# A fused attention and SwiGLU block on one core: gate columns by crossbar-turned weights and VectorE sums, rows spread through DRAM

## The chip, the cores and the metric

The kernel runs on one core of one Trainium2 chip. The metric is the device time of one execution in microseconds (us). Before the change the median of three runs is 1275.24 us (1275.18 to 1275.56).

## The reference

One block of a transformer with conditioning (adaLN), cut to what matters:

```python
mod = (silu(c) @ w_mod).reshape(1, 6, 1, 1024)      # sa, ca, ga, sb, cb, gb
h = layernorm(x) * (1 + ca) + sa
x = x + ga * attention(h)        # wq; 32 query heads on 4 kv heads, last 512 keys; wo
h = layernorm(x) * (1 + cb) + sb
x = x + gb * ((silu(h @ w_gate) * (h @ w_up)) @ w_down)
```

x is 2048 x 1024 in bf16, c is 1 x 1024, w_mod is 1024 x 6144, wq is 1024 x 4096, wo is 4096 x 1024, and the feed-forward width is 3584. The six groups of 1024 numbers in `mod` are the shift, scale and gate of the attention half (sa, ca, ga) and of the feed-forward half (sb, cb, gb).

## The kernel before

**Tiling.** The 2048 rows are worked in four chunks of 512. Attention runs over 128 steps of one (chunk, head) pair each: the loop `for i in range(1, NA + 2)` at line 839, with the 32 heads of chunk 0 in steps 1 to 33. In the steady state step i holds, in TensorE's order, the query projection of head i+3 (`qproj`, eight matmuls of 512 columns into bank QB), the scores of head i-1 (`scores`, four matmuls into four banks, which two exponentials on ScalarE, line 757, empty) and the attention product of head i-2 (`pv`, sixteen matmuls of 129 columns into two banks). VectorE then copies the query projection out (line 640) and, after the product, takes the reciprocal of the sums (line 775) and multiplies (line 778); SyncE issues a crossbar transfer (DMA transpose) that turns the head's output (line 781). After a chunk's last head comes its output projection (`oproj`), whose result is multiplied by a gate row and added to x (`resid`, lines 797 and 799). After all four chunks come gate, up and down projections of the feed-forward half. Steps 1 to 8 are different: the first heads' projections were done before the loop, so that in the odd ones among them no query projection runs.

**Order.** Every engine's instructions are in the order in which the code emits them; there is no planner. `T.op` puts the waits ahead of an instruction by the buffers it reads and writes. SyncE is one in-order queue for nearly all loads, stores and turns: a load that waits holds those behind it. A list of generators, `bg`, gives one piece of background work to each step (`run_bg(1)`): `ln_task` normalises the next chunk in twelve pieces, three empty ones and four that scale and shift. For chunk 1 it starts in step 5.

**The six groups of mod.** sa and ca are made by TensorE at the start. The gate ga is made in chunk 0: two loads of w_mod (`load_wga`, line 562, 1 MB each, steps 2 and 3) and 64 matmuls with one column each (`mod_mm`, called at line 879, in steps 7, 9, 10, 11 and 12). The other three groups, sb, cb and gb, come as 24 columns of 128 in chunks 1 and 2: `load_mt` (line 580) brings a block of w_mod, 1024 x 128, by a DMA transpose into one of two buffers, and four steps later `mod_col` (line 585) multiplies it by the row silu(c) on VectorE and sums along the row.

**Rows.** The gates are needed as rows spread over all partitions (`rowb[0]` for ga, `rowb[1]` for gb), and `mod_col` needs silu(c) so (`sc_row`). `row_task` (line 594) makes such a row from a column tile: GpSimd multiplies the identity matrix by each column (line 600), TensorE multiplies a matrix of ones by these diagonals (eight matmuls of 128 columns in two halves), and VectorE copies the halves out (line 608). It is run three times.

**Loads beside.** In chunk 0 SyncE also issues a 1 MB block of wq every four steps (`load_wq`, line 354, in steps 4, 9, 13, 17, 21, 25 and so on), needed four steps later; eight 1 MB blocks of wo (line 791; steps 5, 7, 10, 12, 15, 18, 20, 23); and a chunk of x (line 299; step 19).

Of the kernel before, what the change touches and what calls it, by code (L numbers as in the profile page):

```python
# [3 lines left out]
ALU = mybir.AluOpType  # L4
AF = mybir.ActivationFunctionType
BF16 = mybir.dt.bfloat16
F32 = mybir.dt.float32
P = 128
# [122 lines left out]
def bass_adaLN_cond__sliding_block_cached__swiglu_ffn__prompt_kernel(  # L131
# [21 lines left out]
    DT = D // P  # L153
# [6 lines left out]
    NJ = 6 * DT  # L160
# [21 lines left out]
    c_row = S_("c_row", [DT, P], BF16)  # L182
    sc_bf = S_("sc_bf", [P, DT], BF16)
    mod_bf = S_("mod_bf", [P, NJ], BF16)
    c6 = S_("c6", [P, DT], F32)
    mcol = S_("mcol", [P, 3 * DT], F32)
    gain = [S_("gain%d" % i, [P, DT], BF16) for i in range(2)]
    gain_f = S_("gain_f", [P, DT], F32)
    nmean = S_("nmean", [P, 1], F32)
# [11 lines left out]
    KB = 1024  # L201
# [7 lines left out]


    OFF_H20 = 154 * KB
    B_ident = _Buf("ident"); B_ones = _Buf("ones"); B_zw = _Buf("zw")
    B_diag = [_Buf("diag%d" % i) for i in range(4)]
    ident = arena.at(OFF_H20, [P], BF16, [B_ident])
    ones_bf = arena.at(OFF_H20 + 256, [P], BF16, [B_ones])
    diag = [arena.at(OFF_H20 + 512 + 256 * i, [P], BF16, [B_diag[i]]) for i in range(4)]
    zwarm = arena.at(OFF_H20 + 2048, [512], BF16, [B_zw])

    def bank(b, n=512, off=0):
        return ps[:, b * 512 + off:b * 512 + off + n]  # L220
# [10 lines left out]
    PB = [_Buf("bank%d" % b) for b in range(8)]  # L231
    B_x = [_Buf("x%d" % t) for t in range(ST)]
    B_mh = _Buf("mhalf")
    B_cT = _Buf("cT"); B_sc = _Buf("sc"); B_late = [_Buf("late%d" % i) for i in range(4)]; B_c6 = _Buf("c6"); B_mcol = _Buf("mcol"); B_scr = _Buf("scr")
    B_mode = _Buf("mode"); B_modc = _Buf("modc"); B_bq = _Buf("bq"); B_gf = _Buf("gf")
    B_nm = _Buf("nmean"); B_acc = _Buf("acc"); B_acc0 = _Buf("acc0")
    B_g = [_Buf("g%d" % i) for i in range(2)]
# [18 lines left out]
    XB = 7  # L256

    with nc.Block() as block:

        @block.gpsimd  # L260
        def _(g):
# [5 lines left out]
            def mm(out_ap, lhsT, rhs, start, stop, reads, bank_buf, skip=False):  # L267
                T.op(PE, lambda: TE.matmul(out_ap, lhsT, rhs, start=start, stop=stop, skip_group_check=skip),  # L268
                     reads=reads, writes=[bank_buf])
# [15 lines left out]
            def finish(gen):  # L285
                while gen in bg:
                    run_bg(1)
# [3 lines left out]
            T.op(POOL, lambda: g.affine_select(out=ident, in_=ident, compare_op=ALU.not_equal,  # L291
                                               fill=1.0, base=0, pattern=[[-1, P]], channel_multiplier=1),
                 reads=[B_ident], writes=[B_ident])
            T.op(POOL, lambda: g.memset(ones_bf, 1.0), writes=[B_ones])
            T.op(POOL, lambda: g.memset(mhalf[:, :], -0.5), writes=[B_mh])
            T.op(POOL, lambda: g.memset(zwarm, 0.0), writes=[B_zw])

            def load_x(ch):
                T.op(Q_x[TPC + ch], lambda: SP.dma_start(
# [156 lines left out]
            def mod_mm(w_ap, wbuf, k, cols):  # L456
                for n, (j, o) in enumerate(cols):
                    mm(bank(XB, 1, 2 * o), w_ap[:, j * P:(j + 1) * P], sc_bf[:, k:k + 1],
                       k == 0 and n == 0, k == DT - 1, [wbuf, B_sc], PB[XB], skip=True)
# [35 lines left out]
            def mod_ca(hf, k):  # L495
# [5 lines left out]
            T.op(PE, lambda: TE.transpose(bank_bf(XB)[:, 0:DT], c_row[:, :], ident[0:DT, 0:DT]),  # L501
                 reads=[B_cT, B_ident], writes=[PB[XB]])
            T.op(ACT, lambda: A.activation(sc_bf[:, :], bank_bf(XB)[:, 0:DT], AF.Silu), writes=[PB[XB], B_sc])
            T.op(ACT, lambda: A.activation(acc[:, 0:1], mhalf[:, 0:1], AF.Exp), reads=[B_mh], writes=[B_acc])


# [47 lines left out]
            norm(2, 2, 2, 512, 512)  # L554


            B_wga = [_Buf("wga%d" % k) for k in range(DT)]
            wga = arena.at(OFF_WO + 48 * KB, [DT, D], BF16, B_wga)
            GCOLS = [(j, j) for j in range(DT)]

            def load_wga(i):
                T.op(dq("q_wga%d" % i), lambda: SP.dma_start(
                    wga[:, i * HK:(i + 1) * HK, :],
                    w_mod[i * HK * P:(i + 1) * HK * P, NE * P:NE * P + D].rearrange("(k p) n -> p k n", p=P)),
                     writes=B_wga[i * HK:(i + 1) * HK])

            NF = NE + DT
            NL = NJ - NF  # L570
            B_mt = [_Buf("mt%d" % i) for i in range(2)]
            mt = [arena.at(OFF_H20 + (2 + 2 * i) * KB, [D], BF16, [B_mt[i]]) for i in range(2)]
            sc_row = arena.at(OFF_H20 + 6 * KB, [D], BF16, [B_scr])
# [2 lines left out]
            def load_mt(n):  # L576
                if n < 2:
                    for b_ in B_qT[NQT:]:
                        B_mt[n].absorb(b_)
                T.op(Q_mt[n % 2], lambda: SP.dma_start_transpose(  # L580
                    mt[n % 2].rearrange("p (a b) -> p a b", a=1), w_mod[:, (NF + n) * P:(NF + n + 1) * P]),
                     writes=[B_mt[n % 2]])

            def mod_col(n):
# [2 lines left out]
                     reads=[B_scr], writes=[B_mt[n % 2], B_mcol])  # L587

            def mod_take(g0, cbuf):
                T.op(DVE, lambda: V.tensor_copy(mod_bf[:, NF + g0 * DT:NF + (g0 + 1) * DT], mcol[:, g0 * DT:(g0 + 1) * DT]),  # L590
                     reads=[B_mcol], writes=[cbuf])


            def row_task(dst, dbuf, src, sbuf):
                T.op(POOL, lambda: g.tensor_copy(c6[:, :], src), reads=[sbuf], writes=[B_c6])

                def diags(n):
                    for q in range(4):
                        col = 4 * n + q
                        T.op(POOL, lambda: g.tensor_scalar(diag[q], ident, c6[:, col:col + 1], None, op0=ALU.mult),  # L600
                             reads=[B_ident, B_c6], writes=[B_diag[q]])

                diags(0)
                yield
                for n in range(2):
                    for q in range(4):
                        mm(bank(XB, P, q * P), ones_bf, diag[q], q == 0, q == 3, [B_ones, B_diag[q]], PB[XB], skip=True)
                    T.op(DVE, lambda: V.tensor_copy(dst[:, n * 512:(n + 1) * 512], bank(XB)),
                         writes=[PB[XB], dbuf])
                    if n == 0:  # L610
                        diags(1)
                    yield


            LEAD = 3
            NQT = 5; NEX = 2; NOS = 4
# [211 lines left out]
            def add_ln2(ch):  # L828
                s = ch % 2
                if ch == 0:  # L830
                    finish(rows)
                    h2s[0] = arena.at(OFF_H20, [DT, CH], BF16, B_h2[0])
                ln2[ch] = ln_task(ch, h2s[s], B_h2[s], 1, 3 * DT, B_late[1])
                bg.append(ln2[ch])

            LOADX = {19: 2, 40: 3}
            LOADT = {Hq + 2 + (9 * n) // 4: n for n in range(NL)}
            LOADO = {5 + (21 * p) // 8: p for p in range(8)}
            for i in range(1, NA + 2):
                ch, h = divmod(i, Hq)  # L840
# [1 line left out]
                    load_wq((i + 4) // 4 + 1)  # L842
                if 2 <= i < NQ0:
                    q_shifted(i)
                if i in (2, 3):
                    load_wga(i - 2)
                if i in LOADX:
                    load_x(LOADX[i])
                if i in LOADO:
# [1 line left out]
                for gk in {2: (1,), 3: (2,), 4: (3,)}.get(i, ()):  # L851
# [3 lines left out]
                    if gk == Hkv - 1:  # L855
                        for b_ in B_hT[1]:
                            for kb in B_kn:
                                b_.absorb(kb)
                if i == 17:
                    bg.append(row_task(sc_row, B_scr, sc_bf[:, :], B_sc))  # L860
                if i == 5:
                    add_ln1(1)
                if h == 2 and 1 <= ch < NCH - 1:
# [3 lines left out]
                if i + LEAD < NA:  # L867
# [7 lines left out]
                        qproj(i + LEAD)  # L875
                    elif i % 2 == 0:
                        qproj(NQ0 - 1 + i // 2)
                for k in {7: (0, 1, 2, 3), 9: (4,), 10: (5,), 11: (6,), 12: (7,)}.get(i, ()):
                    mod_mm(wga[:, k, :], B_wga[k], k, GCOLS)
                    if k == DT - 1:  # L880
                        T.op(DVE, lambda: V.tensor_copy(mod_bf[:, NE:NF], psap(XB * 512, [[2, DT]])), writes=[PB[XB], B_late[0]])
                        rows = row_task(rowb[0], B_row[0], mod_bf[:, NE:NF], B_late[0])
                        bg.insert(0, rows)
                if i - 4 in LOADT:
                    n = LOADT[i - 4]
                    mod_col(n)
                    g0, last = divmod(n, DT)
                    if last == DT - 1:
                        mod_take(g0, B_late[g0 + 1])
                        if g0 == 1:  # L890
                            mod_gain(1, B_late[2], B_g[1])
                        elif g0 == 2:
                            rows = row_task(rowb[1], B_row[1], mod_bf[:, 5 * DT:6 * DT], B_late[3])
                            bg.insert(0, rows)
                if i in LOADT:
                    load_mt(LOADT[i])
                n = i - (NA - LEAD)
# [6 lines left out]
                if 0 <= i - 2 < NA:  # L904
                    pv(i - 2)
                    ch2, h2 = divmod(i - 2, Hq)
                    if h2 == Hq - 1 and ch2 < NCH - 1:
                        finish(rows)
                        oproj(ch2)
                run_bg(1)  # L910

# [148 lines left out]
```

## Time and profile before

| what | value |
|---|---|
| median of three runs | 1275.24 us |
| span of the profiled execution | 1273.8 us |
| TensorE busy, share of the span | 1267.0 us, 99% |
| VectorE / ScalarE / GpSimd busy | 479.6 / 341.5 / 42.0 us |
| DMA, mean | 122 GB/s |
| mean granted TensorE clock | 1.000 |
| a steady attention step | 3.50 us |

A timeline line of the profile reads: start in us from the start of the span, length in us, engine, source line, operation, what it writes and reads, shape, how many are merged, and in brackets how long the engine sat idle before it and what ended that. PE is TensorE's matmuls, PEld its weight loads, DVE is VectorE, ACT is ScalarE, POOL is GpSimd, SPq is SyncE's queue. Matmuls are recorded with overlapping lengths, so their spacing is read from their starts. "Idle before" is only a loss on the engine that sets the end.

### The profile page before, as it was taken

How to read it: one execution, taken by the hardware profiler on the slowest of the kernel's cores; microseconds unless marked ns; L12 is line 12 of the kernel's file. 1: busy time of each engine (PE TensorE's matmuls, PEld its weight loads, DVE VectorE, ACT ScalarE, POOL GpSimd, SP SyncE). 2: the span in 40 equal slices, each digit the busy share in tenths (PEclk: the TensorE clock that was granted, in tenths of full speed). 3: DMA queues.
4: the chain of work that ended last, by engine and by line, in shares of the span. 5: the costliest groups of instructions: out<-in, count | busy, mean ns of one | idle time of the engine just before them, and what ended most of it. 6: DMA issues, size and time to landing. Idle time of an engine off the chain costs nothing.

```text
span 1273.8 us, 17943 instructions
## 1 busy us (share of the span) xinstructions
PE 1267.0 (99%) x7683; PEld 645.7 (51%) x7683; DVE 479.6 (38%) x897; ACT 341.5 (27%) x388; POOL 42.0 (3%) x102
## 2 busy tenths in 40 slices
PE   8999999999999999999999999999999999999999
PEld 5665545555455564455544444444444444444444
DVE  4655315764147652365322331233212331222222
ACT  4555304554025550155510111011100111011100
POOL 1020000000000010000000000000000000000000
PEclk9999999999999999999999999999999999999999
DMA  9999403876018641055253973056411644035200
GB/s 306 271 235 224 99 1 84 194 169 133 1 34 191 140 104 38 5 129 118 67 147 99 285 222 121 25 154 152 148 60 56 192 140 132 17 120 161 66 9 25
DMA packets 235854, 155.31 MB, mean 122 GB/s; under 512 B 129024, under 2 KB 222080, under 8 KB 235776
## 3 DMA queue, kind: packets, MB, share of 16 engines
q1 hardware_dynamic: 177520, 95.45, 30.7%
q10 hardware_dynamic: 58256, 58.73, 14.7%
q8 instruction: 60, 0.98, 0.3%
q14 instruction: 18, 0.15, 0.0%
HBM read 119.54 MB, written 4.19 MB: 97 GB/s over the span
## 4 chain that ended last, share of the span: by engine, by line
PE 99%; DMA 1%; DVE 0%; SPq 0%; ACT 0%; issue 0%
PE ps L268 98%; DMA arena<-in_A_wq_dram 1%; DVE arena L671 0%; SPq L331 0%; SPq L306 0%; PE ps L272 0%; ACT arena L757 0%; DVE arena L666 0%; DVE tmp L797 0%; DVE arena L799 0%; DVE bq L661 0%
## 5 line engine op out<-in xcount | busy, mean ns | idle before, releaser
L268 PE MATMUL ps<-arena 128*128 128x512 bf16 (+1 forms) x7378 | 1260.7, 334 | 4.0 <-POOL arena L408 2.2
L268 PEld LDWEIGHTS ps<-arena 128*128 128x128 bf16 x7378 | 635.6, 98 | 621.0 <-issue 3.9
L757 ACT ACTIVATE arena<-ps 128x1024 bf16<-128x1024 f32 x256 | 261.9, 1023 | 350.3 <-PE ps L268 338.4
L989 ACT ACTIVATE arena<-ps 128x512 bf16<-128x512 f32 x112 | 66.9, 597 | 506.4 <-PE ps L268 506.4
L990 DVE TENSOR_TENSOR arena<-ps,arena 128x512 bf16<-128x512 f32 x112 | 77.4, 691 | 276.6 <-PE ps L268 276.6
L797 DVE TENSOR_TENSOR tmp<-ps,rowb 128x512 f32<-128x512 f32 (+1 forms) x65 | 44.4, 683 | 318.8 <-PE ps L268 318.8
L640 DVE CAST arena<-ps 128x512 bf16<-128x512 f32 x120 | 82.9, 691 | 53.8 <-PE ps L268 53.8
L778 DVE TENSOR_TENSOR arena<-ps,rl 128x512 bf16<-128x512 f32 x128 | 88.5, 691 | 4.7 <-DVE rl L775 0.3
L775 DVE RECIPROCAL rl<-ps 128x4 f32<-128x4 f32 x128 | 23.3, 182 | 118.3 <-PE ps L268 118.3
L415 DVE BATCH_NORM_STATS2 st<-x_res 128x6 f32<-128x512 bf16 x62 | 42.3, 683 | 3.6 <-DMA x_res<-in_A_x_dram 3.5
L420 POOL TENSOR_SCALAR rstd<-mv 128x1 f32<-128x1 f32 x28 | 6.3, 226 | 888.2 <-DVE mv L419 888.2
L585 DVE SCALAR_TENSOR_TENSOR arena<-arena 128x1024 bf16<-128x1024 bf16 x24 | 29.1, 1214 | 0.0
L799 DVE TENSOR_TENSOR arena<-tmp,x_res 128x512 bf16<-128x512 f32 (+1 forms) x33 | 22.3, 675 | 1.1
L799 DVE TENSOR_TENSOR x_res<-tmp,x_res 128x512 bf16<-128x512 f32 x32 | 22.1, 692 | 1.1
L431 DVE TENSOR_SCALAR arena<-arena,gain,mod_bf 128x512 bf16<-128x512 bf16 x56 | 20.3, 404 | 0.0
L426 DVE TENSOR_SCALAR nsc<-x_res,mv,rstd 128x1024 bf16<-128x1024 bf16 x30 | 16.0, 533 | 0.0
L422 POOL TENSOR_TENSOR rstd<-rstd,mhalf 128x1 f32<-128x1 f32 x28 | 15.8, 564 | 2.3
L600 POOL TENSOR_SCALAR arena<-arena,c 128x128 bf16<-128x128 bf16 x24 | 14.4, 616 | 32.7 <-PE ps L268 32.4
L268 PEld LDWEIGHTS ps<-sc_bf,arena 128*128 128x128 bf16 x192 | 6.6, 96 | 2.3 <-DMA arena<-in_w_mod_dram 0.3
L268 PE MATMUL ps<-sc_bf,arena 128*128 128x1 bf16 x192 | 6.8, 163 | 0.0
L419 DVE BATCH_NORM_AGGREGATE mv<-st 128x2 f32<-128x12 f32 x28 | 5.8, 209 | 1.0
L653 DVE COPY arena<-ps 128x512 f32<-128x512 f32 x4 | 2.7, 688 | 8.3 <-PE ps L268 8.3
(53 smaller groups left out, 50.7 us busy)
## 6 DMA issues: line engine op xcount, KB each, us to landing
arena<-in_A_wq_dram SPq DMA_DIRECT2D x31, 1024.0 KB, 6.1
arena<-in_B_w_gate_dram ACTq DMA_DIRECT2D x28, 1024.0 KB, 5.4
arena<-in_B_w_up_dram ACTq DMA_DIRECT2D x28, 1024.0 KB, 8.1
arena<-in_A_wo_dram SPq DMA_DIRECT2D x8, 1024.0 KB, 6.4
arena<-in_B_w_down_dram SPq DMA_DIRECT2D x7, 1024.0 KB, 8.4
out_dram<-arena SPq DMA_DIRECT2D x15, 256.0 KB, 2.0
x_res<-in_A_x_dram SPq DMA_DIRECT2D x3, 1024.0 KB, 6.7
arena<-in_w_mod_dram SPq DMA_DIRECT2D x8, 256.0 KB, 6.3
```

What stands on the lines that cost most here:

```text
L268: T.op(PE, lambda: TE.matmul(out_ap, lhsT, rhs, start=start, stop=stop, skip_group_check=skip), reads=reads, writes=[bank_buf])
L415: T.op(DVE, lambda: V.bn_stats(st_[sl][:, hf * 6:hf * 6 + 6], x_res[:, t, hf * 512:hf * 512 + 512]), reads=[B_x[t]], writes=[B_st[sl]])
L431: T.op(DVE, lambda: V.tensor_scalar(dst[:, dt, :], dst[:, dt, :], gain[gi][:, dt:dt + 1], mod_bf[:, ccol + dt:ccol + dt + 1], op0=ALU.mult ...
L585: T.op(DVE, lambda: V.scalar_tensor_tensor(mt[n % 2], mt[n % 2], 1.0, sc_row, op0=ALU.mult, op1=ALU.mult, accum_out=mcol[:, n:n + 1]), rea ...
L640: T.op(DVE, lambda: V.tensor_copy(qT_s[qs], bank(b)), writes=[PB[b], B_qT[qs]])
L757: T.op(ACT, lambda: A.activation(ex_s[es][:, 2 * kp:2 * kp + 2, :], banks2(SCB + 2 * kp), AF.Exp, scale=att_scale), writes=[PB[SCB + 2 * k ...
L775: T.op(DVE, lambda: V.reciprocal(rl[r][:, :].rearrange("p (a b) -> p a b", a=2), psap(PVB * 512 + P, [[512, 2], [130, 2]])), writes=both + ...
L778: T.op(DVE, lambda: V.tensor_tensor(o_s[os_].rearrange("p (a b) d -> p a b d", a=2), psap(PVB * 512, [[512, 2], [130, 2], [1, P]]), rlb, A ...
L797: T.op(DVE, lambda: V.tensor_tensor(tmp[s][:, 0:n], bank(b, n), rowb[ri][:, c0:c0 + n], ALU.mult), reads=[B_row[ri]], writes=[PB[b], B_tmp ...
L799: T.op(DVE, lambda: V.tensor_tensor(dst[:, c0:c0 + n], tmp[s][:, 0:n], x_res[:, t, c0:c0 + n], ALU.add), reads=[B_tmp[s], B_x[t]], writes= ...
L989: T.op(ACT, lambda: A.activation(sg_s[ss], bank(gb), AF.Silu), writes=[PB[gb], B_sg[ss]])
L990: T.op(DVE, lambda: V.tensor_tensor(guT[:, ft, :], bank(ub), sg_s[ss], ALU.mult), reads=[B_sg[ss]], writes=[PB[ub], B_gu[ft]])
```

## The change

ga's eight columns are made as the other 24 were: eight more loads by DMA transpose (steps 12, 13, 16 to 19, 24, 25) and eight more sums on VectorE (steps 16 to 19 and 24 to 27). `load_wga` and its 64 matmuls go. `row_task` goes with its diagonals, matmuls and copies. A row is now made by writing it to a small DRAM tensor (`row_put`) and reading it back with a step of zero over the partitions (`row_get`); the two gates are first turned from a column tile into rows by a DMA transpose (`row_turn`). silu(c) as rows comes from one more activation on ScalarE. The schedule of the other 24 columns is as before.

```diff
-            T.op(POOL, lambda: g.memset(ones_bf, 1.0), writes=[B_ones])
...
+            T.op(POOL, lambda: g.memset(mstg, 0.0), writes=[B_mstg])
...
+            T.op(ACT, lambda: A.activation(c_sil, c_row[:, :], AF.Silu), reads=[B_cT], writes=[B_csil])
...
-            def load_wga(i):
-                T.op(dq("q_wga%d" % i), lambda: SP.dma_start(
...
-            def row_task(dst, dbuf, src, sbuf):
...
+            def row_put(r, src, sbuf):
+                T.op(Q_dr[r], lambda: SP.dma_start(d_rows[r:r + 1, :].rearrange("o (k p) -> (o k) p", p=P), src),
+                     reads=[sbuf], writes=[B_dr[r]])
+
+            def row_get(r, dst, dbuf):
+                rep_ap = bass.AP(tensor=d_rows.tensor, offset=r * D, ap=[[0, P], [1, D]])
+                T.op(Q_rw[r], lambda: SP.dma_start(dst, rep_ap), reads=[B_dr[r]], writes=[dbuf])
+
+            def row_turn(c0, cbuf):
+                T.op(DVE, lambda: V.tensor_copy(mstg[:, 0:DT], mcol[:, c0:c0 + DT]), reads=[B_mcol], writes=[B_mstg])
+                T.op(Q_turn, lambda: SP.dma_start_transpose(mrow.rearrange("p (a b) -> p a b", a=1), mstg),
+                     reads=[B_mstg], writes=[B_mrow])
...
-            LOADT = {Hq + 2 + (9 * n) // 4: n for n in range(NL)}
+            SUMT = {16: 0, 17: 1, 18: 2, 19: 3, 24: 4, 25: 5, 26: 6, 27: 7}
+            SUMT.update({Hq + 6 + (9 * n) // 4: n + DT for n in range(NL - DT)})
+            LOADT = {12: 0, 13: 1, 16: 2, 17: 3, 18: 4, 19: 5, 24: 6, 25: 7}
+            LOADT.update({Hq + 2 + (9 * n) // 4: n + DT for n in range(NL - DT)})
+            TURNT = {27: 0, max(SUMT): 3}
+            PUTT = {29: 1, max(SUMT) + 2: 2}
+            GETT = {30: 1, max(SUMT) + 3: 2}
...
-                if i in (2, 3):
-                    load_wga(i - 2)
...
-                if i == 17:
-                    bg.append(row_task(sc_row, B_scr, sc_bf[:, :], B_sc))
+                if i == 2:
+                    row_put(0, c_sil, B_csil)
+                if i == 11:
+                    row_get(0, sc_row, B_scr)
...
-                for k in {7: (0, 1, 2, 3), 9: (4,), 10: (5,), 11: (6,), 12: (7,)}.get(i, ()):
-                    mod_mm(wga[:, k, :], B_wga[k], k, GCOLS)
...
-                        finish(rows)
                         oproj(ch2)
```

More of the change, by code (lines that the diff above doesn't have):

```diff
@@ L184, in bass_adaLN_cond__sliding_block_cached__swiglu_ffn__prompt_kernel @@
     mod_bf = S_("mod_bf", [P, NJ], BF16)
-    c6 = S_("c6", [P, DT], F32)
-    mcol = S_("mcol", [P, 3 * DT], F32)
+    mcol = S_("mcol", [P, 4 * DT], F32)
     gain = [S_("gain%d" % i, [P, DT], BF16) for i in range(2)]
@@ L211, in bass_adaLN_cond__sliding_block_cached__swiglu_ffn__prompt_kernel @@
     OFF_H20 = 154 * KB
-    B_ident = _Buf("ident"); B_ones = _Buf("ones"); B_zw = _Buf("zw")
-    B_diag = [_Buf("diag%d" % i) for i in range(4)]
+    B_ident = _Buf("ident"); B_zw = _Buf("zw"); B_csil = _Buf("csil")
+    B_mstg = _Buf("mstg"); B_mrow = _Buf("mrow")
+    B_dr = [_Buf("dr%d" % i) for i in range(3)]
     ident = arena.at(OFF_H20, [P], BF16, [B_ident])
-    ones_bf = arena.at(OFF_H20 + 256, [P], BF16, [B_ones])
-    diag = [arena.at(OFF_H20 + 512 + 256 * i, [P], BF16, [B_diag[i]]) for i in range(4)]
+    mstg = arena.at(OFF_H20 + 256, [P], BF16, [B_mstg])
+    mrow = arena.at(OFF_H20 + 512, [P], BF16, [B_mrow])
+    c_sil = arena.at(OFF_H20 + 768, [P], BF16, [B_csil])[0:DT, :]
+    d_rows = nc.dram_tensor("mod_rows", [3, D], BF16, kind="Internal").ap()
     zwarm = arena.at(OFF_H20 + 2048, [512], BF16, [B_zw])
@@ L233, in bass_adaLN_cond__sliding_block_cached__swiglu_ffn__prompt_kernel @@
     B_mh = _Buf("mhalf")
-    B_cT = _Buf("cT"); B_sc = _Buf("sc"); B_late = [_Buf("late%d" % i) for i in range(4)]; B_c6 = _Buf("c6"); B_mcol = _Buf("mcol"); B_scr = _Buf("scr")
+    B_cT = _Buf("cT"); B_sc = _Buf("sc"); B_late = [_Buf("late%d" % i) for i in range(4)]; B_mcol = _Buf("mcol"); B_scr = _Buf("scr")
     B_mode = _Buf("mode"); B_modc = _Buf("modc"); B_bq = _Buf("bq"); B_gf = _Buf("gf")
@@ L554, in _ @@
             norm(2, 2, 2, 512, 512)
-            B_wga = [_Buf("wga%d" % k) for k in range(DT)]
-            wga = arena.at(OFF_WO + 48 * KB, [DT, D], BF16, B_wga)
-            GCOLS = [(j, j) for j in range(DT)]
-            def load_wga(i):
-                T.op(dq("q_wga%d" % i), lambda: SP.dma_start(
[L563 to L570, printed above, removed]
+            NL = NJ - NE
             B_mt = [_Buf("mt%d" % i) for i in range(2)]
@@ L580, in load_mt @@
                 T.op(Q_mt[n % 2], lambda: SP.dma_start_transpose(
-                    mt[n % 2].rearrange("p (a b) -> p a b", a=1), w_mod[:, (NF + n) * P:(NF + n + 1) * P]),
+                    mt[n % 2].rearrange("p (a b) -> p a b", a=1), w_mod[:, (NE + n) * P:(NE + n + 1) * P]),
                      writes=[B_mt[n % 2]])
@@ L589, in mod_take @@
             def mod_take(g0, cbuf):
-                T.op(DVE, lambda: V.tensor_copy(mod_bf[:, NF + g0 * DT:NF + (g0 + 1) * DT], mcol[:, g0 * DT:(g0 + 1) * DT]),
+                T.op(DVE, lambda: V.tensor_copy(mod_bf[:, NE + g0 * DT:NE + (g0 + 1) * DT], mcol[:, g0 * DT:(g0 + 1) * DT]),
                      reads=[B_mcol], writes=[cbuf])
-            def row_task(dst, dbuf, src, sbuf):
[L595 to L612, printed above, removed]
+            Q_dr = [dq("q_dr%d" % i) for i in range(3)]
+            Q_rw = [dq("q_rw%d" % i) for i in range(3)]
+            Q_turn = dq("q_turn")
+            def row_put(r, src, sbuf):
[8 more added lines that the diff above has]
+                     reads=[B_mstg], writes=[B_mrow])
             LEAD = 3
@@ L877, in _ @@
                         qproj(NQ0 - 1 + i // 2)
-                for k in {7: (0, 1, 2, 3), 9: (4,), 10: (5,), 11: (6,), 12: (7,)}.get(i, ()):
-                    mod_mm(wga[:, k, :], B_wga[k], k, GCOLS)
[L880 to L885, printed above, removed]
+                if i in SUMT:
+                    n = SUMT[i]
                     mod_col(n)
@@ L888, in _ @@
                     if last == DT - 1:
-                        mod_take(g0, B_late[g0 + 1])
-                        if g0 == 1:
+                        if g0 in (1, 2):
+                            mod_take(g0, B_late[g0])
+                        if g0 == 2:
                             mod_gain(1, B_late[2], B_g[1])
-                        elif g0 == 2:
-                            rows = row_task(rowb[1], B_row[1], mod_bf[:, 5 * DT:6 * DT], B_late[3])
-                            bg.insert(0, rows)
+                if i in TURNT:
+                    row_turn(TURNT[i] * DT, B_late[0])
+                if i in PUTT:
+                    row_put(PUTT[i], mrow[0:DT, :], B_mrow)
+                if i in GETT:
+                    row_get(GETT[i], rowb[GETT[i] - 1][:, :], B_row[GETT[i] - 1])
                 if i in LOADT:
@@ L907, in _ @@
                     if h2 == Hq - 1 and ch2 < NCH - 1:
-                        finish(rows)
                         oproj(ch2)
```

## The prediction

> **What bounds the kernel now.** I read the page's busy shares, its slices and its chain first.
>
> ```profile
> PE 1267.0 (99%) x7683; PEld 645.7 (51%) x7683; DVE 479.6 (38%) x897; ACT 341.5 (27%) x388; POOL 42.0 (3%) x102
> ...
> DMA  9999403876018641055253973056411644035200
> ...
> PE 99%; DMA 1%; DVE 0%; SPq 0%; ACT 0%; issue 0%
> ...
> L585 DVE SCALAR_TENSOR_TENSOR arena<-arena 128x1024 bf16<-128x1024 bf16 x24 | 29.1, 1214 | 0.0
> ```
>
> TensorE is the path. The DMA line says that the first four slices (0 to 127 us), where the new transfers go, are full. L585 is the price of one VectorE sum. The chain in order of time has one long piece:
>
> ```profile
> 42.85 1228.07 PE ps L268 x7266
> ```
>
> So a TensorE instruction taken out after 42.85 us shortens the run, unless another engine holds TensorE at that place. I therefore read the timeline where the removed matmuls stand, all engines in order:
>
> ```profile
> 42.84 4.84 PEld L268 LDWEIGHTS ps<-arena 128*128 128x128 bf16 x46 [0.55 <-ACT arena L757]
> ...
> 46.55 2.14 ACT L757 ACTIVATE arena<-ps 128x1024 bf16<-128x1024 f32 x2 [1.59 <-PE ps L268]
> 47.64 0.91 PEld L268 LDWEIGHTS ps<-sc_bf,arena 128*128 128x128 bf16 x32
> 47.69 0.94 PE L268 MATMUL ps<-sc_bf,arena 128*128 128x1 bf16 x32
> ```
>
> The 32 gate-column matmuls of step i=7 lie beside an exponential that ends at 46.55 + 2.14 = 48.69. The first line is step i=5, which has no query projection and where the weight load waited for ScalarE. For the row spreads, the VectorE timeline:
>
> ```profile
> 72.24 0.18 DVE L775 RECIPROCAL rl<-ps 128x4 f32<-128x4 f32 x1 [1.08 <-PE ps L268]
> ...
> 75.96 0.18 DVE L775 RECIPROCAL rl<-ps 128x4 f32<-128x4 f32 x1 [1.08 <-PE ps L268]
> ```
>
> Reciprocals mark the steps: 3.72 us here, 3.50 in a step without extra matmuls. Last, SyncE's timeline at step 16, and the landing times of the 24 existing crossbar loads (L580):
>
> ```profile
> 84.11 1.19 SPq L781 DMA_TRANSPOSE arena<-arena  x1
> 85.40 1.26 SPq L445 DMA_TRANSPOSE arena<-nsc  x1
> 86.79 0.50 SPq L354 DMA_DIRECT2D arena<-in_A_wq_dram  x1
> ```
>
> ```profile
> DMA to landing us min/median/max: 3.2/4.0/6.5
> ```
>
> **Removed from TensorE.** (a) Step 7: 32 one-column matmuls from 47.69 to 48.50, 0.81 us. Without them the four score matmuls start at 47.69, but the third writes the banks that the exponential reads until 48.69. In step 5 the same matmul came 0.06 us after the exponential's end (42.79 to 42.85), so here it starts at 48.75 instead of 48.93: the gain is 0.18, not 0.81. (b) Steps 9 to 12: eight each; these steps take 3.70 instead of 3.50, 4 x 0.20 = 0.81. ScalarE works 2.14 of 3.50 us there and hides nothing. (c) Three row spreads of two halves: 3.72 - 3.50 = 0.22 to 0.23 each, also at 452.89 to 460.33 us, 6 x 0.225 = 1.36. Sum: 0.18 + 0.81 + 1.36 = 2.35 us.
>
> The Trainium skill's page "TensorE: Matmul & The Clock Gate" (Part 1) gives small matmuls two floors: about 25 ns from start to start, and about 62 ns with hardware decode off. By 62 ns, (a) and (b) would have cost 4.0 us. The row above, 0.81 us for 32, is 25 ns each, and the sum goes by it.
>
> **Removed elsewhere.** Six VectorE copies of 0.68 us, 27 GpSimd operations (0.6 us each), and the 2 MB plain load L562: none is on the chain, price nothing. The queue behind that load is short again by 57.9 us, where an output turn lands 3.05 after its issue.
>
> **Added at the start.** One more Silu on ScalarE, near 0.2 us (the one at L503 takes 0.18) before the Exp table load. L508 behind it waited 2.08 us for x, so that hides it; uncovered it costs 0.2. The ones memset gives way to another of its size.
>
> **Added on VectorE.** Eight sums of 1.21 + 0.08 us in steps 16 to 19 and 24 to 27. Without the gate row ahead of them the layer-norm steps come three steps earlier: normalise at 16, nothing at 17 to 19, modulate at 20 to 23, nothing after. A step with a sum then holds cast 0.69, sum 1.29, reciprocal and product 0.9, at most 0.54 more: 3.4 of 3.50. Later chunks already run such steps (205.5 to 223.0 us) at 3.50. Price nothing, if the data are there.
>
> **Added waits.** Each sum waits for its load on VectorE, with the step's reciprocal and product queued behind it, for which the next attention product waits. Load n waits on SyncE for sum n-2 (two buffers), and behind it stand the output turns, wq and wo loads. Loads 2, 3, 6, 7 have two steps (7.0 us) between sums n-2 and n. I place them on the clock of before; by step 16 all queues run 1.45 us ahead alike. One queue holds everything SyncE issues, and landings come in order of issue: the load issued at 239.95, just behind wq, landed 0.83 us after wq; others 0.83 to 0.95.
>
> Load 2: sum 0 ends at 83.3; the load lands by 86.5 to 87.3; sum 2 wants it at 89.0. Fine. Load 3: issued after wq at step 17. With load 2, the output turn and the layer-norm turn ahead, wq goes out near 87.25 and the layer-norm turn lands near 89.1 (3.2 after issue, as now). In this stage wq lands 4.6 to 4.95 behind the transfer ahead of it (88.58 to 93.53 there), so 93.7 to 94.05; load 3 lands 0.83 to 0.95 later, at 94.5 to 95.0. Sum 3 wants it at 91.90 + 0.61 = 92.5: 2.0 to 2.5 us late. The sum, reciprocal and product then end 2.1 us after the landing, and the next product on TensorE was due at 96.27, so lateness up to 1.65 is free. The stall is 0.4 to 0.85; I take 0.7.
>
> Behind it the queue is fuller: wq 94.0, load 3 94.9, turn 95.4, wo 98.1 (+2.7), load 4 and a turn 99.4, x 102.4 (+3.0), load 5 and a turn 103.7, wo and a turn 106.8, wq 111.4 (+4.6). Its heads start at 111.1 plus the stall already taken: no further wait. Load 7 comes behind the wq of step 25 about 1.1 late, under 1.65. Loads 0, 1, 4, 5 have four or six steps.
>
> What a crossbar load takes in this full queue, no row shows. From below 0.83. From above: alone it lands 3.2 after issue, an output turn of half its bytes 2.4, so 128 KB cost 0.8 and the whole 1.6. I take 0.87, the queued rows. At 1.6 load 3 is 0.7 later (stall 1.7), the wq of step 21 has three loads ahead of it and lands 2.2 later, 1.2 beyond what the first stall covers, and load 7, behind loads 6 and wq again, leaves 1.4 more: 4.3 us. From below, no stall.
>
> The page "VectorE: DVE Perf Modes" (The three transpose paths) speaks against the change: 1309 ns for a 128x128 turn by crossbar, 390 on TensorE. A load holds eight such blocks; by 10.5 us each, the four two-step loads would each be 10.5 - 5.7 = 4.8 us late, 3.2 beyond the free 1.65, and the run near 1286 us (an estimate). The rows, 0.83 to 3.2 for a whole load, say otherwise.
>
> **Rows by DRAM.** Three writes of 2 KB, three broadcast reads of 256 KB, two small turns. Stores of 64 KB landed in 1.6 us, 256 KB loads in 3.9. The conditioning row is read at step 11 and used at 16 (17 us). The gate row is turned at 27, put at 29, read at 30, used at the first residual near 149.98 us, six us and more after the read lands. The last has over 200 us. SyncE blocks behind no unfinished one by more than 1 us. Price nothing; a broadcast read has no row, so from nothing to 3 us of queue.
>
> **Sum.** The profiled execution spans 1273.8 us; 1.4 us lie around it to the median of 1275.24. -2.35 + 0.7 = -1.65: 1273.6 us. 0.2% is 2.55 us, about what a measurement of this kernel can tell from no change.
>
> **Rivals.** *Loads in time*: wq lands 3.7 behind, as wo does when it is not deep in the queue. No stall, 1272.9. *ScalarE does not hold step 7*: the whole 0.81 counts and nothing stalls, -2.97, 1272.3; against it speaks step 5. *The queue is the bound* (slower): slices 0 to 3 are full. If a crossbar load takes 2.0 us there, sum 3 is 4.7 late (stall 3.1), the wq of step 21, with three loads ahead, lands 2.0 after its heads want it, and load 7 leaves 2.2 more: 7.3 us, 1280.2. From about 1.7 us a load the run is over 0.2% slower; the bound above is 1.6. *The row goes astray*: the broadcast read is slow and the first residual waits, 3 us or more.
>
> **How the numbers follow.** Forecast (stall 0.3 to 4.3) 0.66; loads in time 0.14, a fifth of it faster by more than 0.2%; step 7 in full 0.09; queue bound 0.09, row 0.02. Faster 0.12, same 0.77, slower 0.11. The range goes from step 7 in full, 1272.3, to the load at 1.6 us, 1275.24 - 2.35 + 4.3 = 1277.2.
>
> **What would show it.** Step 7 shortens by 0.2 us with a wait on ScalarE; steps 9 to 14 take 3.50; step 19 shows L585 waiting 2 us for its load, and the next attention product waits under 1 us. A TensorE wait for wq near 109 us, or crossbar loads landing over 1.6 us behind their predecessors, would make me wrong, as would no wait at all in steps 16 to 28.

## The result and the profile after

The changed kernel takes **1277.39 us** (median of 21 runs, 1276.07 to 1282.22), the kernel before 1275.44 beside it (21 runs, 1275.06 to 1277.0): ratio 1.0017, 95% interval 1.0011 to 1.0023. That is about 2 us slower, within 0.2%; the forecast was 1273.6, and the result lies 0.2 us above the upper end of the range. The profiled execution takes 1276.72 with a span of 1274.4, the shorter end of its runs: the median span of the runs is 1275.0 after and 1273.65 before. The time around the span is 2.23 after and 1.89 before.

The lines of the page that answer to those of before:

```profile
PE 1257.1 (99%) x7454; PEld 641.8 (50%) x7595; DVE 485.1 (38%) x907; ACT 341.6 (27%) x389; POOL 27.0 (2%) x75
...
DMA  9899504866018641065252973055411644035200
...
PE 94%; DMA 3%; DVE 2%; issue 1%; ACT 0%; SPq 0%
...
L575 DVE SCALAR_TENSOR_TENSOR arena<-arena 128x1024 bf16<-128x1024 bf16 x32 | 38.9, 1216 | 5.9 <-DMA arena<-in_w_mod_dram 5.9
```

The matmul line counts 141 fewer than the weight loads (PEld): records that this trace lacks. By the weight loads 88 are gone, the 64 and the 24 that the change removes; most of the 9.9 us by which PE's busy time falls, and the 1% of issue in the chain, come from the missing records. TensorE's share of the chain falls from 99% to 94%, and DMA has 3% where it had 1%. The eight more sums cost 1.22 us each as priced (L575 was L585 before), but VectorE stood 5.9 us in front of them, waiting for gate loads. The chain in order of time, which before was one piece of TensorE, shows where (start, length, what):

```profile
47.30 1.03 ACT arena L743
...
81.49 6.17 DMA arena<-in_w_mod_dram
87.66 0.02 issue
87.68 0.18 DVE arena L575
87.86 5.84 DMA arena<-in_w_mod_dram
...
95.08 0.70 DVE arena L764
95.78 0.05 issue
95.83 4.58 PE ps L270 x44
...
114.76 7.36 DMA arena<-in_w_mod_dram
```

The first line is step 7, which now hangs on ScalarE's exponential, as forecast. The next ones are gate loads 2 and 3, and the last is load 7. Load 3 starts at 87.86 because SyncE comes to it no sooner: its buffer was free when sum 1 had ended, at 84.96, but a wq block stands ahead of it in SyncE's order (the timeline of SyncE is shown below). The chain names sum 2 in front of load 3; by the code load 3 waits for sum 1. On VectorE's timeline, the end of sum 1 and the start of sum 3:

```profile
84.88 0.08 DVE L575 DVE_READ_ACCUMULATOR arena<-arena 128x1 f32 x1
...
93.72 1.23 DVE L575 SCALAR_TENSOR_TENSOR arena<-arena 128x1024 bf16<-128x1024 bf16 x1 [2.90 <-DMA arena<-in_w_mod_dram]
```

What the loads did to the others is in the waits between 60 and 140 us (engine, line, what it waited for: us in total, times, longest us):

```profile
DVE arena L575 <- DMA arena<-in_w_mod_dram: 5.9, 4, 2.9
```

```profile
PEld ps L270 <- DVE arena L764: 2.8, 2, 1.9
```

Of VectorE's 5.9 us, 2.8 reached TensorE's weight loads: twice the attention product waited for VectorE's product (L764), 1.9 after sum 3 and the rest after sum 7. By the spacing of the steps the loss is 2.2, as follows.

Step by step, by the reciprocals of the two traces: the removed matmuls give 0.17 in step 7, 0.20 in each of steps 9 to 12 and 0.22 to 0.23 in each of six row halves, 2.3 in all. Start-up is 0.36 shorter in this execution. Steps 18 to 20 lose 1.56 and steps 26 to 28 lose 0.64. Two losses lie far behind the change: step 66 is 0.60 longer, and the end of the last chunk's attention about 0.4. The sum is +0.5, the spans say +0.6. All this is one execution, one at the shorter end.

### The profile page after: what moved, and what is told of

Read it like the earlier page. It is cut to its first block, busy times and chain, and to the rows that moved or that the text cites. A ratio compares the mean times of both kernels' runs of the same rounds, so it can differ in the third digit from the quotient of the medians.

```text
span 1274.4 us, 17610 instructions
## 1 busy us (share of the span) xinstructions
PE 1257.1 (99%) x7454; PEld 641.8 (50%) x7595; DVE 485.1 (38%) x907; ACT 341.6 (27%) x389; POOL 27.0 (2%) x75
## 4 chain that ended last, share of the span: by engine, by line
PE 94%; DMA 3%; DVE 2%; issue 1%; ACT 0%; SPq 0%
PE ps L270 94%; DMA arena<-in_w_mod_dram 2%; DMA arena<-arena 1%; DVE st L417 0%; DVE arena L575 0%; DVE arena L764 0%; DMA x_res<-in_A_x_dram 0%; PE ps L274 0%; ACT arena L743 0%; DVE arena L657 0%; DVE rl L761 0%; DVE arena L652 0%; DVE nsc L428 0%; DVE arena L626 0%; DVE mv L517 0%
## 5 line engine op out<-in xcount | busy, mean ns | idle before, releaser
L764 DVE TENSOR_TENSOR arena<-ps,rl 128x512 bf16<-128x512 f32 x128 | 88.5, 692 | 4.5
L575 DVE SCALAR_TENSOR_TENSOR arena<-arena 128x1024 bf16<-128x1024 bf16 x32 | 38.9, 1216 | 5.9 <-DMA arena<-in_w_mod_dram 5.9
```

What stands on the lines that cost most here:

```text
L575: T.op(DVE, lambda: V.scalar_tensor_tensor(mt[n % 2], mt[n % 2], 1.0, sc_row, op0=ALU.mult, op1=ALU.mult, accum_out=mcol[:, n:n + 1]), rea ...
L764: T.op(DVE, lambda: V.tensor_tensor(o_s[os_].rearrange("p (a b) d -> p a b d", a=2), psap(PVB * 512, [[512, 2], [130, 2], [1, P]]), rlb, A ...
```

## The experiments

Each was compared with the kernel before on the same chip, whose median was 1275.42 to 1275.61. Three theories stand:

- **T1, lead**: two steps between a gate load's issue and its sum are too short; nothing else is wrong.
- **T2, room**: the one queue that SyncE feeds has no room for 2 MB more in steps 12 to 27; whatever is moved, something comes late until other transfers leave the stretch.
- **T3, the rest**: the loss lies in the rows by DRAM, in VectorE's sums or in something else that the column part brings, not in transfers.

**Rows alone (e2_rows_only).** The kernel before, with its matmul gate columns, and only `row_task` replaced by the write, the broadcast read and the turn.

```diff
-                if i == 17:
-                    bg.append(row_task(sc_row, B_scr, sc_bf[:, :], B_sc))
+                if i == 2:
+                    row_put(0, c_sil, B_csil)
+                if i == 11:
+                    row_get(0, sc_row, B_scr)
...
-                        rows = row_task(rowb[0], B_row[0], mod_bf[:, NE:NF], B_late[0])
-                        bg.insert(0, rows)
...
+                if i == 27:
+                    row_turn(mod_bf[:, NE:NF], B_late[0])
```

> The kernel before with the three rows made through DRAM, and the gate columns still made by 64 TensorE matmuls from the plain load. If the rows by DRAM are free: 24 fewer row matmuls, -1.36 us, 1274.1. If the round trip costs (in the span or outside it): 1275.5 or more. The late-data theory says nothing is lost here, since no crossbar load is in chunk 0.

Measured: 1274.26 us (11 runs), ratio 0.9991 (0.9982 to 1.0), median 1.35 below. Each of the six halves is 0.22 shorter, and no VectorE or TensorE wait for a transfer appears between 60 and 145 us. So the rows were priced rightly: -1.36, and nothing for what they add.

**Columns alone (e3_cols_only).** The kernel before with the eight columns by crossbar and sums, and rows by `row_task` (silu(c)'s moved to step 2, since sums need it from step 16).

```diff
+            SUMT = {16: 0, 17: 1, 18: 2, 19: 3, 24: 4, 25: 5, 26: 6, 27: 7}
...
+            LOADT = {12: 0, 13: 1, 16: 2, 17: 3, 18: 4, 19: 5, 24: 6, 25: 7}
...
-                if i in (2, 3):
-                    load_wga(i - 2)
...
-                if i == 17:
+                if i == 2:
                     bg.append(row_task(sc_row, B_scr, sc_bf[:, :], B_sc))
```

> The kernel before with the eight gate columns by crossbar loads and sums in the changed kernel's steps, and the three rows still by GpSimd diagonals and TensorE. Late data: -0.99 us of matmuls (0.18 + 0.81) + 2.2 us of stalls, 1276.6, with the wide spread of times of the changed kernel. Rows by DRAM at fault: -0.99 and no more than 0.7 back, 1275.1 or less.

Measured: 1280.39 us (5 runs), ratio 1.004 (1.0027 to 1.0052). It overstates the column part: the moved `row_task` costs 1.85 us in step 4, where nothing covers it. Another 0.6 is `row_task` too: the gate row is now spread in step 29, and there TensorE waits 0.5 for GpSimd's diagonals. Beside these artefacts steps 19 and 20 lose 2.1 net and step 66 1.34; sum 7 costs nothing net here. So the stall at sum 3 and the loss at step 66 are there without the rows by DRAM.

**Gate loads left out (e4_no_reload).** The changed kernel without loads 2 to 7. The sums run on the data of loads 0 and 1, so the gate ga is not the reference's; all instructions but the six transfers are there.

```diff
-                if i in LOADT:
+                if i in LOADT and not 2 <= LOADT[i] < DT:
```

> The changed kernel with gate loads 2 to 7 left out: their sums run on what the first two loads left in the two buffers, so the gate is not the reference's. All VectorE work stays, six transfers and their waits go. Late data or full queue: stalls in steps 16 to 28 vanish, near 1273.5 to 1275.2. VectorE's added sums at fault: stalls stay, near 1277.4. Rows by DRAM at fault: at least 1 us over what the removed matmuls promise (1273.1).

Measured: 1274.53 us (11 runs), ratio 0.9991 (0.9982 to 1.0). No transfer is waited for in steps 16 to 28; the gain up to step 30 is 2.10, of which 0.25 is start-up. So the stalls belong to the six transfers and not to the sums, and T3 falls for steps 16 to 28. But 0.67 is lost in step 66 again.

**Loads spread, four steps of lead (e1_spread).**

```diff
-            SUMT = {16: 0, 17: 1, 18: 2, 19: 3, 24: 4, 25: 5, 26: 6, 27: 7}
+            SUMT = {12 + (9 * n) // 4: n for n in range(DT)}
...
-            LOADT = {12: 0, 13: 1, 16: 2, 17: 3, 18: 4, 19: 5, 24: 6, 25: 7}
+            LOADT = {8 + (9 * n) // 4: n for n in range(DT)}
...
-                if i == 11:
+                if i == 5:
                     row_get(0, sc_row, B_scr)
```

> The changed kernel with the eight gate loads in steps 8, 10, 12, 14, 17, 19, 21, 23 and each sum four steps after its load (12 to 27), the conditioning row read back in step 5 instead of 11. Same bytes, same sums, more lead. If the loss is the late data of the loads with two steps of lead: no VectorE wait for these loads over 0.5 us, no TensorE stall in steps 16 to 28, 2.2 us (the 1.56 + 0.64 lost there) less than the changed kernel, so about 0.3 us under the kernel before, and a narrower spread of times. If the full transfer queue itself is the loss: wq or wo blocks come late instead and 1 us or more of TensorE waits stay in chunk 0. If the rows by DRAM cost: nothing moves, near 1277.4.

Measured: 1278.98 us (6 runs, 1274.68 to 1281.37), ratio 1.0024 (1.0011 to 1.0037): no better. VectorE waits for its loads 0.7 us in all. Instead TensorE waits for the wq block of step 21 (issued 105.62, landed 112.67):

```profile
PEld ps L270 <- DMA arena<-in_A_wq_dram: 3.2, 1, 3.2
```

T1 falls: with lead for the loads the wait moves to the transfer behind them. The windows after it show a second price (us; busy time and count of PE, PEld, DVE, ACT, POOL; then the granted clock, the DMA share and GB/s):

```profile
108.00:112.00 4.00, 1.69 (x20) 1.16 (x18) 2.06 (x5) 2.05 (x2) 0.00 (x0) 1.00 1.11 343
112.00:116.00 4.00, 3.28 (x11) 1.32 (x12) 0.70 (x2) 0.00 (x0) 0.00 (x0) 0.73 1.26 244
116.00:120.00 4.00, 4.00 (x29) 2.33 (x28) 2.17 (x5) 2.05 (x2) 0.00 (x0) 0.85 1.17 242
```

At 0.73 and 0.85 of the clock the next 8 us of work lose 4 x 0.27 + 4 x 0.15 = 1.7, so a 3.2 us wait cost 4.88 in step 25.

**Gate load ahead of wq (e7_swap).** Where both are issued in one step, 17 and 25, the order is turned round.

```diff
-                if i % 4 == 1 and i > 5 or i == 4:
+                if (i % 4 == 1 and i > 5 or i == 4) and i not in (17, 25):
                     load_wq((i + 4) // 4 + 1)
...
                     load_mt(LOADT[i])
+                if i in (17, 25):
+                    load_wq((i + 4) // 4 + 1)
```

> The changed kernel with the order on the transfer queue swapped in steps 17 and 25: the gate load goes ahead of the wq block instead of behind it. Late data: the wait of sum 3 (2.9 us) and of sum 7 fall by the four microseconds of a wq block, so no TensorE stall in steps 16 to 28, about 2.2 us less than the changed kernel, 1275.2. Full queue: the wait moves to the wq blocks (of step 21, used in step 25), and 1 us or more of the loss stays, 1276.2 or more.

Measured: 1279.13 us (5 runs), ratio 1.0031 (1.0019 to 1.0044). VectorE's longest wait falls from 2.9 to 1.2, and TensorE waits for wq instead (waits of TensorE's weight loads, 60 to 160 us):

```profile
PEld ps L270 <- DMA arena<-in_A_wq_dram: 4.1, 2, 2.7
```

Order only chooses who waits.

**The x block out of the stretch (e5_x_late, e6_spread_x_late).** The third 1 MB block of x, issued in step 19, goes to step 33; e5 is the changed kernel, e6 the spread one.

```diff
-            LOADX = {19: 2, 40: 3}
+            LOADX = {33: 2, 40: 3}
```

> The changed kernel with the third chunk of x (1 MB) loaded in step 33, when the queue is nearly idle, instead of step 19; nothing else moved. Full queue: the blocks behind it (wo of step 20, wq of step 21, loads 6 and 7) land about 3 us earlier, so the wait of sum 7 and the 0.64 us of steps 26 and 27 go; the 1.56 us of step 19 stay, as load 3 stands ahead of x; 0.6 to 1.2 us less than the changed kernel, 1276.2 to 1276.8. Late data alone, by lead of two steps: load 7 still stands behind a wq block, so nothing changes, 1277.4.

> The spread schedule (each sum four steps after its load, loads in steps 8 to 23) and x in step 33. Full queue: the wq block of step 21 comes 3 us earlier and the 4.9 us lost at step 25 go, all 2.35 us of removed matmuls stay: 1273.3, under the kernel before and under the rows-only kernel (1274.3). If a crossbar load holds the queue for longer than its bytes: at least 2 us of wq waits remain, 1275.5 or more.

Measured: e5 1280.87 us (6 runs), ratio 1.004 (1.0027 to 1.0053); e6 1279.18 (9 runs), ratio 1.0026 (1.0016 to 1.0036). Both were spoilt by a place that I had not priced: step 33 puts x ahead of the last head's turn, which the output projection needs. In e6 x was issued at 140.36 and the turn behind it, issued at 142.00, landed at 150.41 (waits, 60 to 160 us):

```profile
PEld ps L270 <- DMA arena<-arena: 3.2, 1, 3.2
```

That is +2.91 there, +4.88 in e5. But in e6 steps 16 to 28 lose only 0.4, where the changed kernel loses 2.2 and the spread alone 4.9: room in the queue helps, as T2 says. In e5, with lead still short, steps 18 to 20 lose 3.5 net, and a lower clock behind them 1.7.

**The x block behind that turn (e8_x_idle, e9_spread_x_idle, e10_rows_x_idle).** The same move to step 34, in the changed kernel, in the spread one, and, as a control, in rows alone.

```diff
-            LOADX = {19: 2, 40: 3}
+            LOADX = {34: 2, 40: 3}
```

> The changed kernel with one transfer moved: the 1 MB x block of step 19 (the third x block) is issued in step 34, behind the last head's turn of the first chunk, where the output projection runs and the 16 DMA engines are a tenth busy. Queue-is-full theory: loads 2 and 3 stand ahead of x in the queue, so the sum-3 wait of steps 18 to 20 stays (net 1.56 in the profile of the changed kernel); loads 4 to 7 and the wq block of step 21 have 5.6 us of transfer less in front of them, so the net 0.64 of steps 26 to 28 goes: median 1276 to 1277, between the change and the kernel before plus one. Rival (the sums and waits on VectorE are the loss, whatever the queue holds): no different from the change, 1277.4. Since x now follows the last head's turn, steps 33 and 34 lose nothing, unlike when x was in step 33.

> Both moves: gate loads spread over steps 8 to 23 with a lead of four steps to their sums, and the third x block issued in step 34 behind the last head's turn. Queue-is-full theory: with 1 MB less in steps 19 to 27 and the loads no longer two by two, neither a sum nor a wq block is late, and nothing is lost at steps 33 and 34: the priced gains stand whole, 1275.4 - 2.35 = 1273.1, or up to 0.7 more where the wq block ahead of a later chunk's last turn takes 7.0 instead of 5.6: 1273.0 to 1273.8, faster than the rows alone (1274.3). Rival (column sums cost something elsewhere, or the granted clock falls with the added transfers): 1275 or more, with no wait over 1 us in steps 16 to 34 to show for it.

> Control: the kernel before with the three rows by DRAM alone and the same move of the third x block to step 34. Queue-is-full theory: in that kernel nothing waited for a transfer in steps 16 to 28, so the move gives nothing: 1274.3, as the rows alone. Rival (x in step 19 costs something of itself, in any kernel): 1273.5 or less, and then the gain of the run beside it belongs to x and not to the columns.

Measured: e8 1278.46 us (11 runs), ratio 1.0019 (1.001 to 1.0028); e9 1275.41 (11 runs), 1.0002 (0.9993 to 1.001); e10 1274.19 (11 runs), 0.9992 (0.9983 to 1.0001). The control is as rows alone: x in step 19 costs nothing of itself. e8 was a miss: steps 26 to 28 lose 0.1 as expected, but steps 18 to 21 lose 4.7 in its profile, a wait of 3.3 with a lower clock behind it. One megabyte taken out behind loads 2 and 3 does not help these. e9 was half a miss, 3.6 us better than the spread alone, but not the expected 1273.0 to 1273.8. The wq blocks of three steps were still late, 0.6 to 1.2 each (60 to 145 us):

```profile
PEld ps L270 <- DMA arena<-in_A_wq_dram: 2.7, 3, 1.2
```

One move did not make enough room, by these waits. (That a transfer of SyncE's is under way without a gap from 71 to 127 us there says nothing of room: in the kernel before, where nothing waits for a transfer, it is so up to 125 us.) Up to step 32 e6 and e9 issue the same transfers, yet their profiles lose 0.4 and 2.7 in steps 16 to 28. A stall in a single profile can thus be 2 us off, and the medians of several runs carry the argument.

**Two output-weight blocks out as well (e11_room, e12_room_two).** The eight blocks of wo are thinned out, so that two leave for the emptier stretch ahead of the output projection; e11 with spread loads, e12 with the loads of the change.

```diff
-            LOADX = {19: 2, 40: 3}
+            LOADX = {34: 2, 40: 3}
...
-            LOADO = {5 + (21 * p) // 8: p for p in range(8)}
+            LOADO = {5: 0, 7: 1, 10: 2, 14: 3, 18: 4, 22: 5, 26: 6, 30: 7}
```

> Gate loads spread over steps 8 to 23 with four steps to their sums, the third x block in step 34, and the eight blocks of the output weights issued in steps 5, 7, 10, 14, 18, 22, 26 and 30 instead of 5, 7, 10, 13, 15, 18, 20 and 23, so that two of them (2 MB) leave the full stretch for the one from 110 to 145 us, where the DMA share is 0.5 to 0.8. Queue-is-full theory: with the x block alone moved the queue was still never empty from 71 to 127 us and the wq blocks of steps 13, 17 and 21 came 0.6 to 1.2 late each; with two blocks fewer they come in time, and the priced gain stands: 1275.4 - 2.35 = 1273.1, up to 0.7 more where a later chunk's slow wq block stands ahead of its last turn: 1273.0 to 1273.8. Rival (the added crossbar loads slow each 1 MB transfer beside them, at whatever place): the wq blocks stay late, 1275 as with x alone moved.

> The changed kernel, its gate loads and sums in the steps that it has, with the same two moves (x block in step 34, output weights in steps 5, 7, 10, 14, 18, 22, 26 and 30). Queue-is-full theory: load 3 still stands behind the wq block of step 17 and has two steps, 7 us, of which wq and load take 6.5 or more with the wait for the sum of step 17 in front, so 0.5 to 1.5 of the 1.56 at step 19 stays, and the 0.64 at steps 26 to 28 goes: 1273.6 to 1275. Rival (lead alone decides, room does not): 1277.4 as the change.

Measured: e11 **1274.43 us** (11 runs, 1273.68 to 1275.05), ratio 0.9991 (0.9982 to 1.0); e12 1275.86 (11 runs), ratio 1.0004 (0.9995 to 1.0013), 0.9 above its expected range. (The fourth block of wo had been in step 12, not 13 as the expectation says.) e11's groups have no wait left on the sums, and between 60 and 145 us neither TensorE nor VectorE waits for any transfer:

```profile
L575 DVE SCALAR_TENSOR_TENSOR arena<-arena 128x1024 bf16<-128x1024 bf16 x32 | 38.9, 1216 | 0.0
```

The room shows in the windows 70 to 90 and 110 to 150 us (DMA share the last but one), first of the changed kernel, then of e11:

```profile
70.00:90.00 20.00, 19.84 (x162) 11.97 (x163) 14.30 (x28) 11.85 (x12) 0.90 (x3) 1.00 1.12 245
110.00:150.00 40.00, 39.27 (x297) 22.63 (x300) 19.25 (x38) 20.06 (x20) 0.00 (x0) 1.00 0.81 175
```

```profile
70.00:90.00 20.00, 20.00 (x165) 12.03 (x164) 14.41 (x29) 12.21 (x12) 1.25 (x3) 1.00 1.06 217
110.00:150.00 40.00, 40.00 (x293) 22.60 (x292) 18.40 (x35) 18.96 (x19) 0.00 (x0) 1.00 0.89 216
```

TensorE is busy all the time in e11 (the 19.84 of the changed kernel is due to missing records; in its second window there is the stall of sum 7 as well), and the transfers have moved from the first window to the second (in the kernel before the shares are 0.82 and 0.63). e12 shows that both are needed: with the same room but two steps of lead, steps 19 and 20 still lose 1.0 (L575 waits 2.4) and nothing is left of 26 to 28. By medians, with the kernel before at 1275.4 to 1275.6 each time: neither 1277.39, lead alone 1278.98, room alone 1275.86, both 1274.43. T2 stands, with T1 as its second half: the lead is short because a load stands behind a 1 MB block that takes 5.5 us or more.

**What e11 still lacks.** It beats the changed kernel by 3 us, but not rows alone, and it is 0.6 above its expected range. Its profile is 1.9 ahead after the first chunk (the forecast 1.9 up to there: 0.18 + 0.81 + 4 x 0.22). Then step 66 costs 0.56 and the last chunk's end 0.37. Both are alike: the last turn of a chunk stands behind 1 MB loads, and lands later than before. At the last chunk's end these are the first feed-forward weights, issued by ScalarE, and the turn lands 9.3 after its issue, for 8.4 before. At step 66 it is the wq block issued near 309 us, 7.0 instead of 5.6, and the output projection waits for the turn (changed kernel, 300 to 325 us; in the kernel before this view is empty):

```profile
PEld ps L270 <- DMA arena<-arena: 0.9, 1, 0.9
```

That block took 7.0 to 7.2 in each of the ten kernels with both parts, 6.8 with columns alone, and 5.6 to 5.7 in the kernel before and the two with rows alone. The columns thus lose 0.56 + 0.37 = 0.93 of the 0.99 that their 64 matmuls gave, at two places without any changed instruction. Why these blocks are slower was not settled.

## Why the prediction was wrong

**Right.** Step 7 gained 0.17 (forecast 0.18), held by ScalarE. Steps 9 to 12 gained 0.20 each, and the row halves 0.22 to 0.23; rows alone gave 1.35 for 1.36. The sums cost nothing in themselves (e4). Load 3 stood behind wq and was late for sum 3, the lateness passed from VectorE to the next attention product, and load 3 landed 0.86 us after wq, load 7 0.79, for 0.87 in the sum.

**Wrong: the size of the stall at sum 3.** The step "2.0 to 2.5 us late, ... I take 0.7" gave 2.90 and 1.56. It let SyncE issue wq near 87.25 on the clock of before. The changed kernel is 1.8 ahead by then, so 85.4, but SyncE got to it at 87.30 (its timeline; start, length):

```profile
81.49 1.19 SPq L570 DMA_TRANSPOSE arena<-in_w_mod_dram  x1
82.72 1.80 SPq L767 DMA_TRANSPOSE arena<-arena  x1
85.05 2.13 SPq L447 DMA_TRANSPOSE arena<-nsc  x1
87.30 0.51 SPq L356 DMA_DIRECT2D arena<-in_A_wq_dram  x1
87.86 2.00 SPq L570 DMA_TRANSPOSE arena<-in_w_mod_dram  x1
```

The two turns took SyncE 1.80 and 2.13 to issue, where before they took 1.19 and 1.26: 1.5 of the 1.9. I had priced the place that a load takes in the queue, 0.87, but not the time that an issue holds SyncE in a full stretch. Without the six loads the layer-norm turn's issue took 1.24 again (e4). The premise that "all queues run 1.45 us ahead alike" failed already before: SyncE issued the wo block of step 15 at 78.83, where before it was 78.13, after the issue of load 1 had held it for 3.92, and the block landed at 84.66 for 84.02. So while TensorE was ahead, SyncE was behind. Part of this was made good by luck: wq landed 3.21 behind the transfer ahead of it, for 4.6 to 4.95 in the sum, so load 3 came at 93.70 for 92.7 to 93.2 (the predicted 94.5 to 95.0 less 1.8). After sum 3 VectorE's steps were 2.98 late, and step 20 made up 1.42 of it, for the 1.65 that I had taken as free. That the held issues made load 3 late is read from this trace; no run changes them alone. Nor is 1.56 a fixed price: e5 and e8 issue the same up to step 18, and their profiles lose 3.5 and 3.0 in steps 18 to 20. Over the eight gate loads (issue in ns, min/median/max, and us to landing):

```profile
L570 SPq DMA_TRANSPOSE arena<-in_w_mod_dram x8: 1186/1855/3919, 66.8 to 114.8; - x8
...
DMA to landing us min/median/max: 5.8/6.9/8.1
```

The rows of before that I leaned on had 3.2/4.0/6.5 to landing, in chunks where the queue drains between two loads.

**Wrong: "Load 7 ... about 1.1 late, under 1.65".** It cost 0.64: its transfer took 7.36, with the wq block in front taking 7.25 instead of 5.9. Likewise "Load 2: ... Fine" was off by 0.36, the wait of sum 2. "No further wait" for the wq of step 21 held in the changed kernel, where it hid behind the stall of sum 3; in e1, e7 and e9, where sum 3 did not stall, this block or its neighbours came late. So the ending "the queue is the bound" had the mechanism right and the price wrong: it asked for 1.7 us a load, and it decided at 0.8 to 1.1 (seven of the eight loads; load 6 landed 2.3 behind its predecessor), since the load's price is not only its own place in the queue.

**Missed altogether**: 0.6 at step 66 and 0.4 at the end of the last chunk, and 0.3 of time around the span (2.23 for 1.89; 2.06 with rows alone, 2.37 in e11). The median span is 0.6 longer than the profiled one; the runs spread over 6 us after and 2 us before. That this spread comes from single 1 MB transfers taking 5.5 or 7 us is likely, but not shown. The stalls of the profile, 2.2, lie inside the 0.3 to 4.3 that the prediction allowed: 1275.24 - 2.35 + 2.2 would be 1275.1. Of the 2.3 from there to 1277.39, the items of this paragraph are 1.9; the rest is not placed.

The Trainium skill's page "DMA: Bandwidth & Descriptors" (Queues, rings and completion order) says that completion on an issuing engine's queue need not come in order of issue. Here they did: all 43 landings of SyncE's issues between 60 and 130 us in the changed kernel came in order of issue, so a late transfer makes the one behind it late.

## What to carry to other kernels

Work taken off the bounding engine and turned into transfers must be costed against the stretch of the queue in which they are issued: add up what is issued between one needed block and the next, and let others leave that stretch first. Price a transfer three ways: its place in the queue, the time that its issue holds the issuing engine in a full stretch, and the lead of everything behind it. And try the halves of a change apart: here the rows alone, 1274.26 us, give as much as any kernel tried with the columns.

## What the runs showed of the hardware

**The clock after a wait.** Idle stretches of TensorE up to 2.74 us left the granted clock at 1.00 (e6). Four of 2.80 to 3.27 us (e1, e8, two in e5) were followed by 8 us of which two windows had 0.61 to 0.97 of it, costing about 1.7 us each. The page "TensorE: Matmul & The Clock Gate" (Part 1) gives half clock after an idle window of about 3.4 us that runs freely; 1.7 us lost is 3.4 us at half clock, which agrees, and the waits here show that somewhat under 3.4 is enough.

**A 1 MB load does not have one duration.** From 150 us on, outside the full stretch, two thirds of the wq blocks of all fourteen traces take 5.4 to 6.1 us and the others 6.1 to 7.6, two of them 8.3 and 9.0. Some of the slow ones return after one chunk, 168 us: 295 and 309, then 463 and 477 us in the changed kernel; 405, then 572 with rows alone, where those near 295 and 309 take 5.5 and 5.7. Kernels with the same parts have most of them at the same blocks, so it seems to go with the program and not with the execution, though each was profiled once. What decides it is open.

**A crossbar issue can hold SyncE.** Alone it takes 1.19 us; between 70 and 80 us of the changed kernel, at a DMA share of 1.09, one took 3.92. What holds it is not shown.
